# Two u buffers with products spread over the steps, and another order of work from step 95 on, in a kernel of long convolution and a rational-activation MLP

## The chip, the cores and the metric

The kernel runs on one core of one Trainium2 chip. The metric is the device time of one execution in microseconds; the median of several executions stands for a kernel. The profile and the trace come from one execution that the hardware profiler recorded.

## The reference

Two stages follow each other. The first is a long convolution along the sequence, gated twice; the second is an MLP whose activation is a ratio of two polynomials of h and |h|:

```python
h_mlp = np.maximum(pos_emb @ w1, 0.0) @ w2          # (12480, 128)
h_filt = h_mlp * np.exp(-0.01 * pos)[:, None]
u = x * v                                           # (2, 12480, 128)
y = irfft(rfft(u, 2*S, axis=1) * rfft(h_filt, 2*S, axis=0), 2*S, axis=1)[:, :S]
x2 = (x * y).reshape(B * S, D)                      # 24960 rows of 128

h = x2 @ w_in                                       # d_ff = 2048
P = a[0] + a[1]*h + a[2]*h**2 + a[3]*h**3
Q = 1.0 + abs(b[0])*abs(h) + abs(b[1])*h**2
out = (P / (Q + 1e-06)) @ w_out
```

## The kernel before, in words

The convolution is done as transforms on TensorE. The first part of the program (up to about 370 us) makes the filter's spectrum and the whole convolution of batch 0. The second part, `second_part`, runs the MLP over both batches and, beside the MLP of batch 0, the convolution of batch 1.

The MLP's rows are cut into 52 tiles: per batch two halves of 12 tiles of 5 residues (5 x 98 = 490 rows) and one of 4 (392 rows; the narrow tile, every thirteenth). The 2048 hidden units of a tile are done in four parts, so there are 208 steps s = (tile j, part c). A step has four pieces of 128 hidden units, in two halves i = 0, 1 of two pieces each. For a step, the short way of computing (the one that runs here) does this:

- TensorE: `mm1` (L870 to L872) makes half i of h in PSUM, two banks, one per piece; the pool `hp` has two such tiles, one per half in turn.
- ScalarE: `act_v` (L904) makes (h + s)^2 into `v`; `act_q` (L880) makes |h| into `q`; both per half. `act_sq` (L932) squares all four pieces of `q` in place; `act_ln` (L948) takes the logarithm of all four into `l` (one buffer); `act_exp` (L953) makes the first estimate of the reciprocal, per half, into `r` in PSUM (one buffer, two banks).
- VectorE: `dve_v` (L914) finishes the cubic from `v` and h, per half, and is the last reader of that half of h; `dve_e` (L959) and `dve_n` (L964) do one Newton step with `r`, per half.
- GpSimd: `pool_p` (L969) adds a constant to the whole of `v`; `pool_g` (L975) multiplies `v` by `q`, per half.
- TensorE: `mm2` (L987) multiplies by `wout` and adds into `acc`; after the fourth part `store` copies `acc` out on VectorE (L998, L1001) and SyncE's queue writes it.

`q` has three buffers, `v` four. The order of instructions on every engine is written by hand: the string `FIRST` lists the works of a step, each with a delay in steps, and a loop sorts all works of all steps by `s - delay + i / len(order)`. Names end in the half: `d0-1` is `dve_v` of half 0, one step late. `s0`, `s1`, `s2` are three slots per step, in which `slot` does one piece of other work: three of a tile's twelve slots prepare the next tile's input (`attn_a` twice, whose products are L822 on VectorE; `attn_b`, whose cast and difference are L840 and L841), the others run `conv_step`. `tk` takes up what a slot has filled in PSUM.

The convolution of batch 1 goes in 64 groups of two channels, each with three items: s1 (reads u; additions on GpSimd), s2 (product with the spectrum `hg`), s3 (ScalarE copies `qt`, L217, and GpSimd makes `ys`). Its input u = x * v is made in four quarters of 32 channels, `uq`, one buffer. A quarter is eight products on GpSimd (`mult_quarter`, L244) of pieces `xq` and `vq` that SyncE's queue loads (four buffers each), after a memset (`quarter`, L239). `load_step`, called in every slot, does up to two products per call, a next quarter only when all s1 items of the quarter before have been issued; s1 waits in `conv_step` until its quarter is full and READY calls have passed. `load_y` forces the convolution to its end before it is read, about step 97.

`act_q2`, `dve_q3`, `act_sq3` and `pool_q3` are defined and listed in `work`, but no name in `FIRST` calls them:

```python
def act_q2(s):      # ScalarE: |h| of piece 2
def dve_q3(s):      # VectorE: |h| of piece 3, as integer AND 0x7FFFFFFF, PSUM to SBUF
def act_sq3(s):     # ScalarE: square of q, pieces 0 to 2
def pool_q3(s):     # GpSimd: q = q + dl (one input), then q = q * q, piece 3
```

Of the kernel before, what the change touches and what calls it, by code (L numbers as in the profile page):

```python
# [20 lines left out]
N2 = 128  # L21
# [14 lines left out]
UQ = 32  # L36
UC = 16
# [6 lines left out]
CS = 2  # L44
# [4 lines left out]
FIRST = (  # L49
    "v0+0 d1-1 tk+0 m21-3 ln-1 e1-2 q0+0 s1-1 p-1 n1-2 x0-1 m11+0 "  # L50
    "g1-2 q1+0 s2-1 st-3 v1+0 d0+0 tk+0 e0-1 sq+0 m20-2 n0-1 x1-1 "
    "g0-1 s0+0 m10+1 "
)

ATTN = ((1, 2, 4), (1, 3, 5))

# [48 lines left out]
def build(ctx: ExitStack, tc, x, v, pos_emb, w1, w2, w_in, w_out, moe_a, moe_b,  # L105
# [21 lines left out]
    def load_rows(dst, src, t0, k, c0, c, pad, queue=nc.sync):  # L127


        h = N2 // 2  # L130
        if t0 < h < t0 + k:
            load_rows(dst[:, 0:h - t0], src, t0, h - t0, c0, c, pad, queue)
            load_rows(dst[:, h - t0:k], src, h, t0 + k - h, c0, c, pad, queue)
        elif t0 < h:
            queue.dma_start(out=dst[0:M], in_=rows(src, 0, M, t0, k, c0, c))
        else:
            queue.dma_start(out=dst[0:96], in_=rows(src, 0, 96, t0, k, c0, c))
            if pad:
                a = rows(src, 96, 1, t0, k, c0, c)
                queue.dma_start(out=dst[96:98], in_=bass.AP(a.tensor, a.offset, [[0, 2]] + [list(p) for p in a.ap[1:]]))  # L140
            else:
                queue.dma_start(out=dst[96:97], in_=rows(src, 96, 1, t0, k, c0, c))
# [86 lines left out]
    def load_quarter(pool, b, q, n0, bufs):  # L229
        c0 = q * UQ  # L230
        xt = pool.tile([M, UC, UQ], F32, tag="xq", name="xq", bufs=bufs)
        vt = pool.tile([M, UC, UQ], F32, tag="vq", name="vq", bufs=bufs)
        load_rows(xt, xb[b], n0, UC, c0, UQ, False)
        load_rows(vt, vb[b], n0, UC, c0, UQ, True)
        return xt, vt

    def quarter(pool, name, bufs):
        u = pool.tile([M, UQ, N2], F32, tag=name[:2], name=name, bufs=bufs)
        nc.gpsimd.memset(u[96:98, :, H2:], 0.0)  # L239
        return u  # L240

    def mult_quarter(engine, u, n0, xt, vt):
        k = M if n0 < H2 else M - 1
        engine.tensor_tensor(  # L244
            out=u[0:k, :, n0:n0 + UC].rearrange("p c t -> p t c"), in0=xt[0:k], in1=vt[0:k], op=ALU.mult)
# [11 lines left out]
    with ExitStack() as st:  # L257
# [34 lines left out]
        us, uw = {}, []  # L292
# [353 lines left out]
    def second_part(short):  # L646
        st = ExitStack()
# [5 lines left out]
        up = st.enter_context(tc.tile_pool(name="up", bufs=1, reuse_waits="tile"))  # L653
# [57 lines left out]
        us = []  # L711
        pieces = [(q, n0) for q in range(D // UQ) for n0 in range(0, N2, UC)]
        coming = []
        s1_done = [0]

        def load_step():
            for p in us:
                p[2] += p[1] == 0
            for _ in range(2):
                if coming and coming[0][0] * (UQ // CS) <= s1_done[0]:  # L720
                    q, n0, xt, vt = coming.pop(0)
                    if q == len(us):
                        us.append([quarter(up, f"uq{q}", 1), N2 // UC, 0])
                    mult_quarter(nc.gpsimd, us[q][0], n0, xt, vt)
                    us[q][1] -= 1
            while pieces and len(coming) < 4:
                q, n0 = pieces.pop(0)
                coming.append((q, n0) + load_quarter(up, 1, q, n0, 4))

        items = conv_items()  # L730
        item = [next(items)]
# [2 lines left out]
        def take_up():  # L734
            if taken[0] is not None:
                fn, t = taken[0]
                taken[0] = None
                fn(t)
# [7 lines left out]
        def conv_step(now):  # L746
            if item[0] is None:
                return
            kind, ready, fetch, work = item[0]
            if kind != now:  # L750
                return
            if ready is not None and not ready():
                return
            if fetch is not None:
                fetch()
            issue(*work)
            item[0] = next(items, None)
# [7 lines left out]
        def load_y(j):  # L765
            if j >= len(tiles):
                return
            b, p0, _ = tiles[j]
            p0 = chunk(p0)
            if (b, p0) in yc:  # L770
                return
            while b and item[0] is not None:
                load_step()
                conv_step(item[0][0])
            take_up()
            n = min(YC, H2 - p0 % H2)
            t = mp.tile([K1, NY, 2, YC, CY], F32, tag="yc", name="yc", bufs=1)
            o = 0 if j else NPT
            nc.sync.dma_start(out=t[:, :, :, o:n, :].rearrange("p g r t c -> p g r (t c)"),
                              in_=y_d[b][:, :, :, p0 + o:p0 + n, :].rearrange("p g r t c -> p g r (t c)"))  # L780
            yc[b, p0] = t
# [8 lines left out]
        def load_xg(j):  # L790
            if j >= len(tiles):
                return
            b, p0, n = tiles[j]
            xt = mp.tile([M, NPT, D], F32, tag="xt", name="xt", bufs=2)
            load_rows(xt[:, 0:n], xb[b], residue(p0, n), n, 0, D, True)
            gt = mp.tile([K1, NPT, 2, M], F32, tag="gt", name="gt", bufs=2)
            nc.sync.dma_start(out=gt[:, 0:n], in_=g_d[:, p0:p0 + n])
            xg[j] = (xt, gt)
# [5 lines left out]
        def attn_a(j, q):  # L804

            b, p0, n = tiles[j]
            yt = yc[b, chunk(p0)] if j else y0
            xt, gt = xg[j]
            i0 = q * NA
            i1 = min(n, i0 + NA)  # L810

            def fill(cv):
                for i in range(i0, i1):
                    k = i if p0 < H2 else n - 1 - i
                    for r in range(2):
                        nc.tensor.matmul(out=cv[0:M, 0, (i - i0) * D:(i - i0 + 1) * D], lhsT=gt[:, k, r, :],  # L816
                                         rhs=yt[:, :, r, p0 - chunk(p0) + k, :], start=(r == 0), stop=(r == 1))

            def take(cv):
                if q == 0:  # L820
                    an[j] = mp.tile([M, NPT, D], F32, tag="an", name="an", bufs=1)
                nc.vector.tensor_tensor(  # L822
                    out=an[j][:, i0:i1, :], in0=cv[0:M, 0, 0:(i1 - i0) * D].rearrange("p (t c) -> p t c", c=D),
                    in1=xt[:, i0:i1, :], op=ALU.mult)
            issue(fill, take)

        def attn_b(j):
            n = tiles[j][2]
            w = n * M
            take_up()  # L830
            t = an.pop(j)

            def fill(cv):
                for i in range(n):
                    nc.tensor.transpose(out=cv[:, 0, i * M:(i + 1) * M], in_=t[:, i, :], identity=ident[0:M, 0:M])

            def take(cv):
                hi = mp.tile([D, NPT * M], F32R, tag="ahi", name="ahi", bufs=2)
                lo = mp.tile([D, NPT * M], F32R, tag="alo", name="alo", bufs=2)
                nc.vector.tensor_copy(out=hi[:, 0:w], in_=cv[:, 0, 0:w])  # L840
                nc.vector.tensor_tensor(out=lo[:, 0:w], in0=cv[:, 0, 0:w], in1=hi[:, 0:w].bitcast(F32), op=ALU.subtract)  # L841
                ah[j] = (hi, lo)
            issue(fill, take)
# [170 lines left out]

        def slot(s, k):

            load_step()
            j, c = steps[s]
            i = 3 * c + k
            if i == 0:  # L1020
                at[:] = ATTN[item[0] is None]
            if j + 1 < len(tiles) and i in at:
                q = at.index(i)
                if q == 2:
                    attn_b(j + 1)
                else:
                    attn_a(j + 1, q)
                return
            take_up()
            if i == at[2] + 1:  # L1030
                load_xg(j + 2)
                load_y(j + 2)
            conv_step((i - sum(i > k for k in at)) % 3)
# [19 lines left out]
                "qa": act_q2, "qd": dve_q3, "sr": act_sq3, "pq": pool_q3}  # L1053
        plan = []
        for s in range(ns):
            order = FIRST.split()
            for i, w in enumerate(order):
                name, delay = w[:-2], int(w[-2:])
                plan.append((s - delay + i / len(order), s, name))
        for _, s, name in sorted(plan):  # L1060
            if name in work:
                work[name](s)
# [4 lines left out]
    with tc.If(rv > 0) as cmp:  # L1067
        second_part(True)
    with cmp.Else():
        second_part(False)  # L1070
# [26 lines left out]
```

## Time and profile before

| | us |
|---|---|
| median of 3 runs | 2366.91 (2366.55 to 2369.27) |
| profiled execution | 2364.71 |
| its span | 2362.9 |
| TensorE matmul busy | 2038.9 (86%) |
| VectorE busy | 2033.5 (86%) |
| ScalarE busy | 2028.6 (86%) |
| GpSimd busy | 1827.9 (77%) |
| mean granted TensorE clock | 0.97 |

In the rows below, PE is TensorE, DVE VectorE, ACT ScalarE and POOL GpSimd; L followed by a number is a line of the kernel. A row of a window gives the busy time of each engine in a stretch of the span, in microseconds, with the number of instructions. A row of the timeline gives an instruction's start and duration, and in brackets the idle time before it and what ended that. A row of grouped instructions gives their number, busy time, and the mean of one in nanoseconds. Instructions of one engine overlap a little at their ends, so what one costs in a row of others is the distance of the starts.

### The profile page before, as it was taken

What the parts mean: (1) busy time and instruction counts of PE and PEld (TensorE: products, weight loads), DVE (VectorE), ACT (ScalarE), POOL (GpSimd) and SP (SyncE); (2) the same over time, 40 slices, a digit from 0 to 9 for tenths busy, and PEclk for the clock granted to TensorE, in tenths of its full rate; (3) what the DMA queues carried; (4) which work ended last, traced back from release to release, by engine and by line L of the source; (5) the groups of instructions that cost most, each with busy time, mean ns of one, the idle gap of its engine ahead of it and who ended that gap; (6) DMA issues with size and microseconds to landing.
All of it is one profiled execution on the core that took longest, in us unless ns stands there. A gap on an engine that the chain in (4) does not pass through costs nothing.

```text
span 2362.9 us, 35120 instructions
## 1 busy us (share of the span) xinstructions
PE 2038.9 (86%) x13344; PEld 1799.9 (76%) x13344; DVE 2033.5 (86%) x2261; ACT 2028.6 (86%) x1971; POOL 1827.9 (77%) x1274
## 2 busy tenths in 40 slices
PE   6899886999899989998999898887788878877787
PEld 4677774888788878887888777776777767777775
DVE  7999984899799978998999888888888888888886
ACT  5322225999899989998999999999999999999997
POOL 4588765899899998999999766667666766767666
PEclk9999997999999999999999999999999999999999
DMA  7465428322522262314321201212021122120210
GB/s 151 102 148 131 119 76 136 75 63 66 99 66 60 64 102 60 76 54 93 74 63 43 54 21 40 45 31 45 17 44 38 27 44 45 31 45 15 46 24 10
DMA packets 357834, 150.20 MB, mean 64 GB/s; under 512 B 292518, under 2 KB 339880, under 8 KB 354776
## 3 DMA queue, kind: packets, MB, share of 16 engines
q1 hardware_dynamic: 350632, 124.10, 25.9%
q10 hardware_dynamic: 7024, 23.76, 3.2%
q8 instruction: 107, 1.75, 0.3%
q14 instruction: 71, 0.58, 0.1%
HBM read 99.65 MB, written 48.17 MB: 63 GB/s over the span
## 4 chain that ended last, share of the span: by engine, by line
ACT 57%; PE 16%; DVE 15%; POOL 5%; issue 4%; DMA 2%; SPq 1%; DVEq 0%; POOLq 0%; ACTq 0%
ACT v L904 13%; ACT q L880 12%; ACT l L948 11%; ACT r L953 11%; ACT q L932 9%; PE acc L987 4%; DVE v L914 2%; DVE q L959 2%; PE cv L816 2%; DVE q L964 2%; PE cs L582 2%; PE cs L150 2%; POOL v L975 1%; PE h L870 1%; PE h L871 1%
## 5 line engine op out<-in xcount | busy, mean ns | idle before, releaser
L975 POOL TENSOR_TENSOR v<-v,q 128x980 f32<-128x980 f32 (+1 forms) x416 | 936.6, 2252 | 356.1 <-DVE q L964 346.4
L987 PE MATMUL acc<-wout,v 128*128 128x128 f32 (+2 forms) x6656 | 845.4, 280 | 79.5 <-DVE ot L1001 48.1
L987 PEld LDWEIGHTS acc<-wout,v 128*128 128x128 f32 (+2 forms) x6656 | 803.0, 190 | 126.8 <-POOL v L969 53.1
L914 DVE SCALAR_TENSOR_TENSOR v<-v,sc,h 128x980 f32<-128x980 f32 (+1 forms) x416 | 505.2, 1214 | 138.1 <-ACT q L880 132.2
L959 DVE SCALAR_TENSOR_TENSOR q<-q,sc,r 128x980 f32<-128x980 f32 (+1 forms) x416 | 504.9, 1214 | 73.8 <-ACT r L953 73.7
L964 DVE SCALAR_TENSOR_TENSOR q<-q,r 128x980 f32<-128x980 f32 (+1 forms) x416 | 482.2, 1159 | 14.4
L870 PE MATMUL h<-ahi,win_l 128*128 128x490 f32 (+1 forms) x832 | 366.7, 441 | 143.3 <-DVE v L914 138.3
L904 ACT ACTIVATE v<-h,sc 128x980 f32<-128x980 f32 (+1 forms) x416 | 454.4, 1092 | 33.2 <-PE h L872 31.4
L880 ACT ACTIVATE q<-h 128x980 f32<-128x980 f32 (+1 forms) x416 | 415.0, 998 | 20.0 <-PE h L872 14.1
L953 ACT ACTIVATE r<-l 128x980 f32<-128x980 f32 (+1 forms) x416 | 418.4, 1006 | 12.5 <-DVE q L964 12.5
L932 ACT ACTIVATE q<-q,sc 128x1960 f32<-128x1960 f32 (+1 forms) x208 | 404.8, 1946 | 0.0
L948 ACT ACTIVATE l<-q,sc 128x1960 f32<-128x1960 f32 (+1 forms) x208 | 400.9, 1928 | 0.0
L969 POOL TENSOR_SCALAR v<-v,sc 128x1960 f32<-128x1960 f32 (+1 forms) x208 | 392.8, 1888 | 0.1
L871 PE MATMUL h<-alo,win_h 128*128 128x490 f32 (+1 forms) x832 | 324.5, 390 | 0.0
L872 PE MATMUL h<-ahi,win_h 128*128 128x490 f32 (+1 forms) x832 | 323.3, 389 | 0.0
L870 PEld LDWEIGHTS h<-ahi,win_l 128*128 128x128 f32 x832 | 160.6, 193 | 187.0 <-DVE v L914 134.3
L872 PEld LDWEIGHTS h<-ahi,win_h 128*128 128x128 f32 x832 | 161.2, 194 | 26.8
L871 PEld LDWEIGHTS h<-alo,win_h 128*128 128x128 f32 x832 | 161.8, 195 | 14.0 <-DVE alo L841 0.4
L816 PE MATMUL cv<-yc,gt 90*98 90x128 f32 x1004 | 127.8, 274 | 1.5 <-DVE ta L162 0.9
L816 PEld LDWEIGHTS cv<-yc,gt 90*98 90x98 f32 x1004 | 117.4, 166 | 5.7 <-DVE an L822 1.3
L589 ACT ACTIVATE qt<-cs 90x512 f32<-90x512 f32 x64 | 34.5, 589 | 97.9 <-PE cs L582 97.9
L582 PEld LDWEIGHTS cs<-idfth,yy 128*90 128x90 f32 x512 | 61.2, 165 | 32.5 <-issue 25.5
(110 smaller groups left out, 2346.3 us busy)
## 6 DMA issues: line engine op xcount, KB each, us to landing
yc<-y_d SPq DMA_DIRECT2D x23, 900.0 KB
gt<-in_g_dram SPq DMA_DIRECT2D x48, 344.5 KB
h_d<-hg ACTq DMA_DIRECT2D x32, 360.0 KB
y_d<-ys ACTq DMA_DIRECT2D x16, 720.0 KB
hg<-h_d SPq DMA_DIRECT2D x64, 180.0 KB
y_d<-ys SPq DMA_DIRECT2D x16, 720.0 KB
xq<-in_x_dram SPq DMA_DIRECT2D x32, 196.0 KB
vq<-in_v_dram SPq DMA_DIRECT2D x32, 196.0 KB
```

Source lines behind the costliest of these rows:

```text
L870: nc.tensor.matmul(out=t[:, k, 0:w], lhsT=wl, rhs=hi[:, 0:w], start=True, stop=False)
L871: nc.tensor.matmul(out=t[:, k, 0:w], lhsT=wh, rhs=lo[:, 0:w], start=False, stop=False)
L880: nc.scalar.activation(out=halves(st_q[s], i, width(s)), in_=st_h[s, i], func=AF.Abs, **({} if short else {"scale": col("b0")}))
L904: nc.scalar.activation(out=v, in_=st_h[s, i], func=AF.Square, bias=col("s"))
L914: stt(out=v, in0=v, scalar=col("k"), in1=h, op0=ALU.add, op1=ALU.mult)
L932: nc.scalar.activation(out=q, in_=q, func=AF.Square, bias=col("dl"))
L948: nc.scalar.activation(out=part(st_l, s, i), in_=part(st_q, s, i), func=AF.Ln, **({"bias": col("ka")} if short else {}))
L953: nc.scalar.activation(out=t[:, :, 0:w], in_=halves(st_l[s], i, w), func=AF.Exp, scale=-1.0)
L959: nc.vector.scalar_tensor_tensor(out=q, in0=q, scalar=col("ka") if short else 0.0, in1=st_r[s, i], op0=ALU.add, op1=ALU.mult)
L964: nc.vector.scalar_tensor_tensor(out=q, in0=q, scalar=2.0, in1=st_r.pop((s, i)), op0=ALU.subtract, op1=ALU.mult)
L975: nc.gpsimd.tensor_tensor(out=v, in0=v, in1=halves(st_q[s], i, w), op=ALU.mult)
L987: nc.tensor.matmul(out=acc[j][0:k, q // 128, :], lhsT=g[:, i, q:q + k], rhs=wout[:, f, :], start=(f == 0 and q == 0), stop=(f == NF - 1), ...
```

## The change

It adds a second string, `REST`, that holds for the steps from 95 on, moved by 1.875 steps against `FIRST`. In `REST` the second abs is split: ScalarE does piece 2 (`qa`), VectorE piece 3 (`qd`); ScalarE squares pieces 0 to 2 (`sr`), GpSimd piece 3 (`pq`, two instructions); `pool_p` is done in two halves (`p0`, `p1`). The order of the works on every engine is another one; ScalarE's is qa, x0, sr, v1, v0 of the next step, x1, q0 of the next step, ln. Up to step 94 `FIRST` stays. `uq` gets a second buffer, so that a quarter may be filled while the quarter before is still read; after the first quarter, products come one a step (slot 0) instead of two a slot; `xq` and `vq` have three buffers instead of four.

```diff
+REST = (
+    "g0-2 e1-2 p0-1 qa+0 s1+1 n1-2 d0+0 g1-2 qd+0 x0-1 p1-1 e0-1 "
+    "m20-2 m10+1 s2+1 pq+0 sr+0 v1+0 n0-1 d1+0 s0+2 v0+1 m21-2 x1-1 "
+    "q0+1 tk+0 m11+1 tk+0 ln+0 st-2 "
+)
+SHIFT, SWITCH = 1.875, 95
...
-        def load_step():
+        def load_step(k=0):
             for p in us:
                 p[2] += p[1] == 0
-            for _ in range(2):
-                if coming and coming[0][0] * (UQ // CS) <= s1_done[0]:
+            for _ in range(2 if not us or us[0][1] else int(k == 0)):
+                if coming and (coming[0][0] - 1) * (UQ // CS) <= s1_done[0]:
                     q, n0, xt, vt = coming.pop(0)
                     if q == len(us):
-                        us.append([quarter(up, f"uq{q}", 1), N2 // UC, 0])
+                        us.append([quarter(up, f"uq{q}", 2), N2 // UC, 0])
                     mult_quarter(nc.gpsimd, us[q][0], n0, xt, vt)
                     us[q][1] -= 1
-            while pieces and len(coming) < 4:
+            while pieces and len(coming) < 3:
                 q, n0 = pieces.pop(0)
-                coming.append((q, n0) + load_quarter(up, 1, q, n0, 4))
+                coming.append((q, n0) + load_quarter(up, 1, q, n0, 3))
...
         def slot(s, k):
-            load_step()
+            load_step(k)
...
         for s in range(ns):
-            order = FIRST.split()
+            order, shift = (FIRST, 0) if s < SWITCH else (REST, SHIFT)
+            order = order.split()
             for i, w in enumerate(order):
                 name, delay = w[:-2], int(w[-2:])
-                plan.append((s - delay + i / len(order), s, name))
+                plan.append((s - delay + shift + i / len(order), s, name))
```

## Rows read from the trace of the kernel before

**Rows 1.** Windows: eleven wide tiles, and step 95 to the last logarithm; columns as printed.

```profile
core 0: us, PE busy (x) PEld busy (x) DVE busy (x) ACT busy (x) POOL busy (x), PEclk, DMA share, GB/s
...
1325.83:2343.00 1017.17, 834.97 (x5576) 745.20 (x5576) 852.50 (x836) 1006.97 (x896) 707.33 (x336) 0.97 0.16 34
1402.48:1809.86 407.38, 331.99 (x2207) 298.30 (x2206) 341.24 (x331) 403.38 (x353) 282.19 (x133) 0.97 0.17 36
```

**Rows 2.** Timeline of ScalarE in one step: start, duration (us), instruction.

```profile
1800.76 1.94 ACT L948 ACTIVATE l<-q,sc 128x1960 f32<-128x1960 f32 x1
1802.57 1.00 ACT L880 ACTIVATE q<-h 128x980 f32<-128x980 f32 x1
1803.44 1.01 ACT L953 ACTIVATE r<-l 128x980 f32<-128x980 f32 x1
1804.35 1.01 ACT L880 ACTIVATE q<-h 128x980 f32<-128x980 f32 x1
1805.21 1.11 ACT L904 ACTIVATE v<-h,sc 128x980 f32<-128x980 f32 x1
1806.17 1.97 ACT L932 ACTIVATE q<-q,sc 128x1960 f32<-128x1960 f32 x1
1807.99 1.03 ACT L953 ACTIVATE r<-l 128x980 f32<-128x980 f32 x1
```

**Rows 3.** Timeline of VectorE in the same step.

```profile
1803.60 1.23 DVE L914 SCALAR_TENSOR_TENSOR v<-v,sc,h 128x980 f32<-128x980 f32 x1 [1.25 <-ACT q L880]
1804.75 1.23 DVE L959 SCALAR_TENSOR_TENSOR q<-q,sc,r 128x980 f32<-128x980 f32 x1
1806.02 1.17 DVE L964 SCALAR_TENSOR_TENSOR q<-q,r 128x980 f32<-128x980 f32 x1
1807.11 1.23 DVE L914 SCALAR_TENSOR_TENSOR v<-v,sc,h 128x980 f32<-128x980 f32 x1
```

**Rows 4.** Windows: the three refills of u, then fifteen plain steps with convolution.

```profile
622.92:651.75 28.83, 21.16 (x133) 19.27 (x134) 17.12 (x20) 18.72 (x18) 24.78 (x18) 0.88 0.95 144
851.65:868.45 16.80, 10.68 (x50) 9.51 (x51) 8.78 (x9) 8.34 (x9) 16.80 (x15) 0.70 0.89 124
1071.01:1087.31 16.30, 11.18 (x67) 9.68 (x68) 11.46 (x13) 9.85 (x11) 16.30 (x14) 0.90 0.96 164
918.39:1061.64 143.25, 137.84 (x978) 126.83 (x979) 134.84 (x135) 142.92 (x133) 134.34 (x114) 1.00 0.23 58
```

**Rows 5.** Groups of GpSimd instructions by shape, whole run: busy us, mean ns, idle before.

```profile
L975 POOL TENSOR_TENSOR v<-v,q 128x980 f32<-128x980 f32 x384 | 876.9, 2284 | 327.4 <-DVE q L964 318.1 <-ACT q L932 5.8
L969 POOL TENSOR_SCALAR v<-v,sc 128x1960 f32<-128x1960 f32 x192 | 367.6, 1915 | 0.1
L244 POOL TENSOR_TENSOR uq<-xq,vq 97x512 f32<-97x512 f32 x16 | 20.3, 1299 | 4.1 <-DMA vq<-in_v_dram 4.1
L455 POOL TENSOR_TENSOR win_l<-f,win_h 128x256 fp32r<-128x256 f32 x8 | 15.2, 1902 | 1.4 <-ACT win_h L460 1.4
L239 POOL MEMSET uq<- 2x2048 f32 x4 | 7.2, 1802 | 0.2
```

**Rows 6.** ScalarE's copy of `qt`, grouped by shape, 389 to 1330 us.

```profile
L217 ACT ACTIVATE qt<-cv 90x512 f32<-90x512 f32 x64 | 39.3, 615 | 0.0
```

**Rows 7.** VectorE's passes for the next tile and the store, by shape, from 1400 us.

```profile
L841 DVE TENSOR_TENSOR alo<-cv,ahi 128x490 fp32r<-128x490 f32 x23 | 15.4, 669 | 0.8
L840 DVE CAST ahi<-cv 128x490 fp32r<-128x490 f32 x23 | 15.2, 661 | 0.0
L998 DVE COPY ot<-acc 128x384 f32<-128x384 f32 x26 | 14.3, 549 | 0.0
L822 DVE TENSOR_TENSOR an<-cv,xt 98x384 f32<-98x384 f32 x25 | 13.7, 549 | 0.0
L822 DVE TENSOR_TENSOR an<-cv,xt 98x256 f32<-98x256 f32 x23 | 9.6, 416 | 0.0
L1001 DVE COPY ot<-acc 106x128 f32<-106x128 f32 x24 | 6.7, 280 | 0.0
```

**Rows 8.** Waits in all, 1600 to 2000 us: us in total, times, longest.

```profile
DVE v L914 <- ACT q L880: 41.2, 43, 1.3
```

## The prediction

> **What bounds the kernel now.** I read the windows by stage first, then one step on ScalarE and VectorE, then the waits. A step is one pass of the loop over (tile, quarter of the hidden units). Its logarithm on ScalarE (L948) marks it, and I count steps by that. From step 104 to 148, eleven wide tiles, 407.38 us pass: 37.03 a tile, 9.26 a step, and ScalarE is busy 403.38 of them [rows 1]. VectorE has 341.24 (7.76 a step) and GpSimd 282.19 (6.41), so GpSimd idles 2.85 us a step. From step 95 to the last logarithm it is 1017.17 us for 112 steps, ScalarE busy 1006.97.
>
> ScalarE's step in order of time [rows 2] has its instructions start one right behind the other: logarithm 1.81 (1800.76 to 1802.57), abs 0.87, exp 0.91, abs 0.86, square of h 0.96, square of q 1.82, exp 0.91, and the square of h again 0.96: 9.10 in all. Four such steps are 36.4, so a tile loses about 0.6 to waits. What ScalarE does is what a step costs. On VectorE [rows 3] the passes follow each other after 1.15 (`dve_v`), 1.27 (`dve_e`) and 1.09 (`dve_n`), twice a step: 7.02.
>
> In the first 95 steps ScalarE also copies `qt` for the convolution of batch 1. Fifteen plain steps there take 143.25 us, 9.55 each, and GpSimd is busy 134.34 of them, so only 0.59 a step is spare [rows 4]. Three short stretches are much longer: 28.83 us for two steps, 16.80 and 16.30 for one each. In them ScalarE is busy only 18.72, 8.34 and 9.85, while GpSimd works almost throughout (24.78, 16.80, 16.30) [rows 4]: the single `uq` buffer is refilled, eight products of 1.30 us and a memset of 1.80 [rows 5], all in one burst in front of the step's own GpSimd work.
>
> **The change, part by part.** *ScalarE, from step 95.* The second abs falls from two pieces to one, the square of q from four to three. A ScalarE pass over 512 columns (`qt`) takes 615 ns [rows 6] against 1.00 for 980 [rows 2], which starts the next after 0.87; so 0.46 for one piece, 0.40 saved. A quarter of 1.82 is 0.455. Together 0.85; with no fixed cost at all it would be 0.89, and 0.70 if the whole 0.615 of the short pass counts. ScalarE's step is then 8.25, a tile 33.0.
>
> *VectorE, from step 95.* One more pass, 490 columns from PSUM to SBUF as integers. No row shows that operation. The cast of 490 columns from PSUM takes 661 ns, a two-input pass of 490 takes 669 [rows 7]; below, half of the 1.09 that a 980-column pass needs, 0.55; above, the 1.23 of a whole one. I take 0.66, of which 0.08 overlaps the next: 0.58. VectorE's step is 7.60. Per tile come two products (0.55 and 0.42), a cast and a difference (0.66 and 0.67) and the store's copies (0.55 and 0.28) [rows 7]: 3.13, about 2.65 with overlap. A tile on VectorE is then 30.4 + 2.65 = 33.05. **The two engines become equal.** By the new order both products fall into one step (about 8.4), the cast pair into the next (8.80), the copies into a third (8.27), and the fourth is ScalarE's 8.25. If nothing carries over between steps, that is 33.7; if all does, 33.05. Today's order loses 0.6 a tile although VectorE has spare time, so I lean to the upper end and take 33.9.
>
> *GpSimd, from step 95.* A one-input pass over 490 (a quarter of 1.92: 0.48) and a product (half of 2.28: 1.14) [rows 5]: 1.62. Its two half additions instead of one whole add next to nothing. 6.41 + 1.62 = 8.03, inside 8.25 to 8.5. The cover is its idle time, which is nearly used up. The logarithm now waits for this square too. In the new order VectorE's abs stands right behind the first `dve_v`, the GpSimd square follows after `p1`, and by the gaps above it ends more than a microsecond ahead of the logarithm; I cost the wait at nothing. If GpSimd is late, ScalarE's whole queue stands behind the logarithm.
>
> The Trainium skill speaks against this move: "GPSIMD Engine Reference", section "Engine selection", has VectorE do elementwise work because GpSimd is about half as fast with two inputs. By that the square belongs on VectorE, where about 0.6 more would make VectorE's step 8.2 and its tile some 35.5; the rows decide for GpSimd, because here it has 2.85 us free and VectorE has not.
>
> *A new wait in PSUM.* VectorE waited 41.2 us, 43 times of up to 1.3, with `dve_v` for ScalarE's abs [rows 8], though it uses nothing of that abs: what they share is the h tile. So readers of one bank go one after the other, in program order. "PSUM — Partial Sum Buffer" of the Trainium skill, section "PSUM bank collisions raise a hardware error", says that two engines must not touch one bank in the same cycle, reads included; the wait agrees. Hence ScalarE's `v1`, which reads both pieces, now waits for VectorE's abs. In steady state x1's end, then `e1`, `n1`, the first `dve_v` and the abs (1.27 + 1.09 + 1.15 + 0.66 = 4.2) must fit ahead of `v1`, while ScalarE does q0, logarithm, abs, exp and square of q (0.87 + 1.81 + 0.46 + 0.91 + 1.37 = 5.4). About a microsecond is left; the cast pair (1.33) uses it up in one step of four. TensorE's next h product, queued behind, has as much room.
>
> *Sum from step 95.* 112 steps are 25 wide tiles and 3 narrow ones. 37.03 - 33.9 = 3.13, times 25: 78. For narrow ones, whose fixed costs don't shrink, I take half, 1.5 each: 4.5. Together **83 us less**. Ends: 33.05 a tile gives 105, 35.2 (8.80 in every step) gives 48. The switch itself, where the pipeline is laid anew, I put at 3 us; at most one step, 9, at least 0.
>
> *The second buffer.* The first quarter's fill is unchanged: two products a call, and DMA decides. The other three refills cost today 28.83 - 19.10 = 9.7, then 7.25 and 6.75: 23.7 us. Afterwards the same work per quarter (8 x 1.30 + 1.80 = 12.2) comes one product a step. Eight steps have 8 x 0.59 = 4.7 to spare; 7.5 is left over. The bursts of today also bring 12.2 and stall for 7.9 on average, so the queue soaks up 4.3, some 0.9 of it spare time; 3.4 is slack of the buffers. The refill then still stalls for about 4, once less because the convolution has barely begun. Together some 10, so **14 us less**, between 1 (no slack, 3 x 7.5) and 24. The loads come three ahead instead of four, and at one piece a step that is three steps ahead; behind them on SP's queue stand `hg`, `xt`, `gt` and the stores, which were behind the bursts before. I cost that at nothing. The convolution ends some steps earlier, its sum unchanged.
>
> *Sum.* 83 + 14 - 3 = 94. The profiled execution took 2364.71 us (span 2362.9), the median of the runs is 2366.91, 2.2 above. I take the difference off the median: **2273 us**.
>
> **Rivals.** *(a) The two engines alternate instead of overlapping.* `r` has one buffer: exp, `dve_e`, `dve_n`, exp. With VectorE full, each late `dve_n` holds ScalarE, and every step becomes as long as the worst, 8.80: 48 + 14 - 3 = 59, 2308 us. For: a tile loses 0.6 today already. Against: without extras VectorE has 0.65 to spare.
>
> *(b) The second buffer brings nothing.* GpSimd lacks the time however the products are spread, stalls only move: 83 + 1 - 3 = 81, 2286 us. For: 0.59 spare a step against 1.3. Against: the burst hits the buffers' slack once, the spread uses eight steps.
>
> *(c) The abs holds `v1` in every step* [rows 8], TensorE's next h product comes late, and ScalarE stays near 9.2: only the buffer counts, 2353 us. Against: the microsecond worked out above.
>
> *(d) Slower.* GpSimd becomes the bound at the new square. A two-input pass on 256 elements took 1.90 in the weight split (L455) [rows 5], three times the rate of `pool_g`; at that rate 490 cost 3.64, with the addition 4.12. A step is then 6.41 + 4.12 = 10.5, 1.27 longer than 9.26: 112 x 1.27 = 142 more, less 14, 2495 us. It decides from 2.85 us for the two new instructions on. Against: that row writes the rounded type; `pool_g`, float like the square, is the nearer one.
>
> **Chances.** Forecast 0.56, (a) 0.20, (b) 0.14, (c) 0.05, (d) 0.05. The range takes in the forecast's ends and (a) and (b): 2246 (33.05 a tile and most of the buffer's gain, 105 + 17 - 1 = 121) to 2313 ((a) with 9 for the switch, 59 - 6 = 53). Outside are (c), (d) and the far ends. Faster by over 0.2% (about what a measurement of this kernel tells from no change) 0.93, within it 0.02, slower 0.05.
>
> **What would show it.** Late tiles of 33.5 to 34.2 us between logarithms; ScalarE busy 8.2 a step, VectorE's share up from 84% to about 98% and GpSimd's from 69% to about 95%; an integer pass of about 0.66 on VectorE; square and addition on GpSimd at 1.6 together; no long burst of `uq` products, and steps of about 10 instead of 16 while a quarter is filled. Wrong would be: ScalarE idle over 0.5 a step in front of the logarithm (GpSimd late), `v1` (abs late) or the exps (a); or GpSimd above 8.3 a step (d).

## The result, and the profile after

The changed kernel takes 2274.71 us (median; 2271.58 to 2275.97), the one before 2366.73 in the same comparison: ratio 0.9608, 95% interval 0.9594 to 0.9623, so 92 us less. The forecast was 2273 with a range of 2246 to 2313. The profiled execution took 2275.51, its span is 2273.6; against that of before 89 us less. In the changed kernel's profile every line below the new string stands six lines later (L948 of before is L954); the new L948 and L949 are GpSimd's two instructions, L899 is VectorE's abs, L893 and L943 are ScalarE's abs of one piece and square of three.

Windows of the changed kernel, in the columns of [rows 1]. First 44 steps of wide tiles (from step 105) and step 95 to the last logarithm, as [rows 1]; then, as [rows 4], steps 24 to 26, which are plain, step 27, step 47 and fifteen plain steps; last, step 94.

```profile
core 0: us, PE busy (x) PEld busy (x) DVE busy (x) ACT busy (x) POOL busy (x), PEclk, DMA share, GB/s
...
1403.72:1771.85 368.13, 325.05 (x2208) 280.94 (x2207) 360.89 (x375) 367.76 (x354) 363.87 (x265) 1.00 0.19 40
1322.24:2252.40 930.16, 818.62 (x5528) 702.64 (x5528) 900.97 (x945) 919.75 (x896) 908.37 (x669) 1.00 0.17 37
624.94:653.50 28.56, 27.54 (x195) 24.62 (x194) 27.18 (x29) 28.47 (x28) 28.42 (x24) 1.00 0.53 96
653.50:669.55 16.05, 12.10 (x68) 11.34 (x67) 9.31 (x10) 9.84 (x10) 16.05 (x15) 0.79 0.59 122
850.73:865.17 14.44, 10.52 (x72) 10.20 (x71) 8.77 (x9) 9.04 (x10) 14.44 (x14) 0.88 0.55 106
914.25:1057.57 143.32, 137.85 (x977) 126.80 (x978) 134.88 (x135) 142.98 (x133) 134.40 (x114) 1.00 0.25 63
1303.90:1322.24 18.34, 16.17 (x104) 14.78 (x104) 11.12 (x12) 10.66 (x10) 13.87 (x9) 0.91 0.26 47
```

The 112 late steps fell from 1017.17 to 930.16, 87.0 less; a wide tile from 37.03 to 33.47 (368.13 / 11). In it ScalarE is busy 99.9%, GpSimd 98.8% and VectorE 98.0% of the time: three engines end within 2% of each other. Step 94, where one order gives way to the other, takes 18.34 instead of 9.12. The plain steps of the convolution are what they were (143.32 against 143.25). Of the long steps of the refills two are left, 27 and 47, with GpSimd working throughout; a third no longer appears.

One late step, first on ScalarE, then on GpSimd (timeline: start, duration; the x2 are v1 and the next step's v0).

```profile
1420.35 1.97 ACT L954 ACTIVATE l<-q,sc 128x1960 f32<-128x1960 f32 x1
1422.17 0.62 ACT L893 ACTIVATE q<-h 128x490 f32<-128x490 f32 x1
1422.63 1.04 ACT L959 ACTIVATE r<-l 128x980 f32<-128x980 f32 x1
1423.54 1.57 ACT L943 ACTIVATE q<-q,sc 128x1470 f32<-128x1470 f32 x1
1424.96 2.09 ACT L910 ACTIVATE v<-h,sc 128x980 f32<-128x980 f32 x2
1426.88 1.05 ACT L959 ACTIVATE r<-l 128x980 f32<-128x980 f32 x1
1427.79 1.05 ACT L886 ACTIVATE q<-h 128x980 f32<-128x980 f32 x1
1428.66 1.99 ACT L954 ACTIVATE l<-q,sc 128x1960 f32<-128x1960 f32 x1
```

```profile
1417.70 0.70 POOL L948 TENSOR_SCALAR q<-q,sc 128x490 f32<-128x490 f32 x1
1418.48 1.00 POOL L949 TENSOR_TENSOR q<-q 128x490 f32<-128x490 f32 x1
1419.44 2.30 POOL L981 TENSOR_TENSOR v<-v,q 128x980 f32<-128x980 f32 x1
1421.71 1.09 POOL L975 TENSOR_SCALAR v<-v,sc 128x980 f32<-128x980 f32 x1
1422.76 2.32 POOL L981 TENSOR_TENSOR v<-v,q 128x980 f32<-128x980 f32 x1
1425.03 1.11 POOL L975 TENSOR_SCALAR v<-v,sc 128x980 f32<-128x980 f32 x1
1426.09 0.71 POOL L948 TENSOR_SCALAR q<-q,sc 128x490 f32<-128x490 f32 x1
```

ScalarE starts one instruction right behind the other, 8.31 from logarithm to logarithm (against 9.10 in [rows 2]): the abs of one piece costs 0.46, the square of three 1.42. GpSimd too has no gap over 0.08, and its round, from 1417.70 to 1426.09, is 8.39. That is **longer than ScalarE's**. Up to step 134 most steps take 8.30, and in each of them GpSimd falls behind by 0.09, of which the one step of 8.49 in a tile gives 0.1 back: at step 109 its square ends 0.88 ahead of the logarithm that reads it, at step 135 only 0.10. By then the slack is used up, and the four steps from 135 on take 8.40, 8.39, 8.46 and 8.31, together 33.56, which is four of GpSimd's rounds. The narrow tile gives the slack back (the lead is 2.78 at step 155), and the same begins again. Four rows of step 135 show how GpSimd holds ScalarE (timeline of each engine; the last is v0 of the next step):

```profile
1654.29 2.30 POOL L981 TENSOR_TENSOR v<-v,q 128x980 f32<-128x980 f32 x1
1656.65 2.04 PE L993 MATMUL acc<-wout,v 128*128 128x128 f32 x16 [1.02 <-POOL v L981]
1659.65 0.38 PE L878 MATMUL h<-ahi,win_h 128*128 128x490 f32 x1
1660.08 1.08 ACT L910 ACTIVATE v<-h,sc 128x980 f32<-128x980 f32 x1
```

TensorE stands idle for 1.02 until GpSimd's product is there, and makes the next h only behind that product's multiplication. That h ends at 1660.03, and ScalarE's v0, which reads it, starts 1.04 behind v1 instead of 0.96. So GpSimd reaches ScalarE through TensorE's queue. The delay is not idle time in the rows, because ScalarE's instructions overlap by about 0.1; a busy share of 99.9% therefore does not prove that nothing waits.

Grouped by shape, in late steps (GpSimd 1400 to 1780 us; VectorE to 2250): number, busy us, mean ns.

```profile
L975 POOL TENSOR_SCALAR v<-v,sc 128x980 f32<-128x980 f32 x91 | 99.0, 1088 | 0.0
L949 POOL TENSOR_TENSOR q<-q 128x490 f32<-128x490 f32 x46 | 46.1, 1003 | 3.8
L948 POOL TENSOR_SCALAR q<-q,sc 128x490 f32<-128x490 f32 x46 | 31.6, 688 | 0.0
```

```profile
L899 DVE TENSOR_SCALAR q<-h 128x490 int32<-128x490 int32 x94 | 62.1, 660 | 0.2 <-ACT q L893 0.2
```

VectorE's abs has the length of the cast it was costed by [rows 7], 0.66. GpSimd's addition on a quarter is 0.69, not the 0.48 of a quarter of 1.92; its square 1.00, not 1.14; and two half additions to `v` take 2 x 1.09 where one whole took 1.92 [rows 5].

### The profile page after: what moved, and what is told of

It is laid out like the page before. It is cut to its first block, busy times and chain, and to the rows that moved or that the text cites. A ratio compares the mean times of both kernels' runs of the same rounds, so it can differ in the third digit from the quotient of the medians.

```text
span 2273.6 us, 35833 instructions
## 1 busy us (share of the span) xinstructions
PE 2026.0 (89%) x13344; PEld 1758.5 (77%) x13344; DVE 2083.5 (92%) x2374; ACT 1942.7 (85%) x1971; POOL 2037.5 (90%) x1613
## 4 chain that ended last, share of the span: by engine, by line
POOL 36%; ACT 25%; PE 22%; DVE 10%; issue 3%; DMA 2%; SPq 2%; POOLq 0%; DVEq 0%; ACTq 0%
POOL v L981 19%; POOL v L975 9%; PE acc L993 6%; ACT v L910 6%; ACT l L954 5%; ACT r L959 5%; ACT q L886 4%; POOL q L949 4%; ACT q L938 3%; POOL q L948 2%; PE cv L822 2%; PE cs L588 2%; PE cs L156 2%; PE h L876 2%; PE h L877 2%
## 5 line engine op out<-in xcount | busy, mean ns | idle before, releaser
L993 PEld LDWEIGHTS acc<-wout,v 128*128 128x128 f32 (+2 forms) x6656 | 774.3, 186 | 193.7 <-POOL v L981 168.4
L910 ACT ACTIVATE v<-h,sc 128x980 f32<-128x980 f32 (+1 forms) x416 | 438.5, 1084 | 31.6 <-PE h L878 30.3
L975 POOL TENSOR_SCALAR v<-v,sc 128x980 f32<-128x980 f32 (+3 forms) x321 | 422.7, 1317 | 0.0
L954 ACT ACTIVATE l<-q,sc 128x1960 f32<-128x1960 f32 (+1 forms) x208 | 401.3, 1929 | 0.9 <-POOL q L949 0.7
L876 PE MATMUL h<-ahi,win_l 128*128 128x490 f32 (+1 forms) x832 | 360.6, 433 | 29.7 <-DVE v L920 27.2
L877 PE MATMUL h<-alo,win_h 128*128 128x490 f32 (+1 forms) x832 | 319.5, 384 | 0.0
L878 PE MATMUL h<-ahi,win_h 128*128 128x490 f32 (+1 forms) x832 | 317.4, 382 | 0.0
L886 ACT ACTIVATE q<-h 128x980 f32<-128x980 f32 (+1 forms) x303 | 302.6, 999 | 8.9 <-PE h L878 6.2
L938 ACT ACTIVATE q<-q,sc 128x1960 f32<-128x1960 f32 (+1 forms) x95 | 185.8, 1955 | 0.0
L943 ACT ACTIVATE q<-q,sc 128x1470 f32<-128x1470 f32 (+1 forms) x113 | 170.9, 1513 | 0.0
L949 POOL TENSOR_TENSOR q<-q 128x490 f32<-128x490 f32 (+1 forms) x113 | 111.4, 986 | 9.4
```

Of the source, the lines that this page charges most:

```text
L876: nc.tensor.matmul(out=t[:, k, 0:w], lhsT=wl, rhs=hi[:, 0:w], start=True, stop=False)
L877: nc.tensor.matmul(out=t[:, k, 0:w], lhsT=wh, rhs=lo[:, 0:w], start=False, stop=False)
L878: nc.tensor.matmul(out=t[:, k, 0:w], lhsT=wh, rhs=hi[:, 0:w], start=False, stop=True)
L910: nc.scalar.activation(out=v, in_=st_h[s, i], func=AF.Square, bias=col("s"))
L954: nc.scalar.activation(out=part(st_l, s, i), in_=part(st_q, s, i), func=AF.Ln, **({"bias": col("ka")} if short else {}))
L975: nc.gpsimd.tensor_scalar(out=v, in0=v, scalar1=col("p0" if short else "a0"), scalar2=1.0, op0=ALU.add, op1=ALU.mult)
```

## The experiments

### The two halves of the change by themselves

Only the buffers:

```diff
-SHIFT, SWITCH = 1.875, 95
+SHIFT, SWITCH = 1.875, 208
```

> Only the buffers and the spread products; the order of work is the old one to the end. Theory (the buffer gives about 13 us, the order about 87 less 9 at the switch): 2367 - 13 = 2354 us; late tiles 37.0 as before, the long steps 27 and 47 as in the changed kernel. Rival (the second buffer brings nothing, stalls only move): 2365 to 2367.

Measured: 2351.87 us against 2367.45, ratio 0.9934 (0.9917 to 0.9950), 15.6 less. Steps 27 and 47 take 15.99 and 13.88, a late tile 37.04, with the same four steps as before (9.12, 9.11, 9.11, 9.70). The buffer does what was forecast, and the rival falls.

Only the order:

```diff
-            for _ in range(2 if not us or us[0][1] else int(k == 0)):
-                if coming and (coming[0][0] - 1) * (UQ // CS) <= s1_done[0]:
+            for _ in range(2):
+                if coming and coming[0][0] * (UQ // CS) <= s1_done[0]:
...
-                        us.append([quarter(up, f"uq{q}", 2), N2 // UC, 0])
+                        us.append([quarter(up, f"uq{q}", 1), N2 // UC, 0])
...
-            while pieces and len(coming) < 3:
+            while pieces and len(coming) < 4:
...
-                coming.append((q, n0) + load_quarter(up, 1, q, n0, 3))
+                coming.append((q, n0) + load_quarter(up, 1, q, n0, 4))
```

> Only the new order from step 95; one u buffer and bursts of products as before. Theory: 2367 - 87 + 9 = 2289 us, late tiles 33.5, the three long refills of before (28.8, 16.8, 16.3) back. Rival (the order needs the earlier end of the convolution, so that steps 95 on are disturbed): above 2295.

Measured: 2289.76 us, ratio 0.9669 (0.9652 to 0.9685), 77.7 less; step 94 takes 17.94, the next 8.29 and 8.30, so the order does not need the earlier end of the convolution. The long refills are back (27.94 for two steps, then 15.78 and 16.48). 15.6 + 77.7 = 93.3 against 92.0 for both: the halves add, neither needs the other.

### What the step at the switch is made of

```diff
-SHIFT, SWITCH = 1.875, 95
+SHIFT, SWITCH = 0.875, 95
```

> The changed kernel with the new order moved by 0.875 steps instead of 1.875, so that its first works stand one step earlier in every queue. Theory (step 94 takes 18.3 instead of 9.1 because the h product of step 95 stands on TensorE behind the last products of steps 93 and 94, which wait for GpSimd): most of the 9 us goes, 2275 - 6 = 2269, between 2266 and 2272. Rival (the 9 us is the price of filling the new pipeline, wherever it starts): 2275, the same; or the later works are now in the way and it is slower.

Measured: 2271.24 us (2268.29 to 2273.02), 3.5 less than the changed kernel, at the upper edge of what the theory gave; the ranges of the two kernels' runs overlap a little, so the total alone does not settle it. The windows are plainer: steps 93 to 95, in the changed kernel and then here.

```profile
1295.00:1330.54 35.54, 25.47 (x156) 23.06 (x154) 26.16 (x29) 27.46 (x26) 22.88 (x15) 0.88 0.39 74
```

```profile
1292.64:1322.69 30.05, 25.50 (x162) 23.28 (x161) 26.20 (x29) 27.46 (x27) 23.34 (x15) 0.89 0.45 88
```

The same work, ScalarE busy 27.46 in both, in 5.5 us less. ScalarE's idle time in these three steps falls from 8.1 to 2.6. So a good half of the 9 us came from where the first works of the new order stand in the queues, and the rest stays. What stands in the way is what the theory said: in step 94 of the changed kernel TensorE's first product for h starts only at 1311.24, behind two groups of `mm2` that waited 2.36 and 0.63 for GpSimd, and ScalarE waits 4.5 us for h in that step, against 1.3 in these three steps with the earlier start.

### Whether the long steps are GpSimd's load

```diff
-            for _ in range(2 if not us or us[0][1] else int(k == 0)):
+            for _ in range(2 if not us or us[0][1] else int(k == 0 and s % 2 == 0)):
```

(with s handed to `load_step` by `slot`)

> The changed kernel with a product of u only in every second step after the first quarter. Theory (GpSimd has 0.59 us a step to spare, a product takes 1.3, so that one a step overfills it and one in two steps does not quite, with the buffers' slack of 3 to 4 us per quarter): steps 27 and 47 fall from 16.0 and 14.4 to below 11, together 9 to 11 us, 2265 us. Rival (the long steps come from something else than GpSimd's load, such as the stores and loads on SyncE's queue, 9.9 us for eight stores at step 26): they stay, 2275.

Measured: 2265.09 us, ratio 0.9570 (0.9554 to 0.9586), 9.6 less than the changed kernel. Windows of steps 26 and 27, and of 47:

```profile
641.56:660.75 19.19, 18.61 (x130) 16.98 (x129) 18.11 (x17) 19.19 (x20) 19.19 (x19) 1.00 0.37 84
841.53:850.43 8.90, 8.05 (x60) 7.41 (x58) 8.16 (x9) 8.81 (x10) 8.90 (x9) 1.00 0.00 0
```

Both long steps are gone. GpSimd works throughout steps 26 and 27 and ScalarE too: the load only just fits. The stores on SyncE's queue are unchanged, so they were not the cause. The loads of pieces come half as often as well, but in the changed kernel GpSimd worked throughout step 27 (16.05 of 16.05) and did not wait for them. Steps 50 and 51, at the narrow tile with convolution, take 10.20 and 10.10 here as in the changed kernel, with ScalarE waiting for h: that is not the refill. Steps 48 and 49 ahead of them take 10.23 and 10.40 here instead of 9.12 and 8.88, so of the 5.5 saved at step 47 2.6 come back.

### Whose time a late step is

*No work moved, the new order kept:*

```diff
-    "g0-2 e1-2 p0-1 qa+0 s1+1 n1-2 d0+0 g1-2 qd+0 x0-1 p1-1 e0-1 "
-    "m20-2 m10+1 s2+1 pq+0 sr+0 v1+0 n0-1 d1+0 s0+2 v0+1 m21-2 x1-1 "
+    "g0-2 e1-2 p0-1 q1+0 s1+1 n1-2 d0+0 g1-2 x0-1 p1-1 e0-1 "
+    "m20-2 m10+1 s2+1 sq+0 v1+0 n0-1 d1+0 s0+2 v0+1 m21-2 x1-1 "
```

> The changed kernel, its new order from step 95, but no work moved: ScalarE does the abs of both pieces and the square of all four, VectorE's abs and GpSimd's two instructions are gone. Theory (a late step costs what ScalarE does in it, 8.30 with the moved work): 8.30 + 0.40 + 0.455 = 9.15 a step, 112 x 0.85 = 95 more, 2370 us. Rival (part of the gain is the order itself, shorter waits between the engines): 2330 to 2350.

Measured: 2350.85 us, between the two forecasts and next to the rival's. The step is what the theory gave, 9.11, with ScalarE busy without a gap:

```profile
1408.00:1800.00 392.00, 314.29 (x2159) 279.24 (x2157) 334.39 (x321) 392.00 (x344) 287.31 (x172) 1.00 0.18 37
```

But the tile's slip is gone: 36.55 (9.22, 9.11, 9.12, 9.11) where the old order with the same work took 37.03. That is the order's own part: the 112 late steps take 1004.9 against 1017.2, so 12.3 of the 87.0 are the order and 74.7 the moved work. Step 94, 20.20 here, takes 11 back; hence the same time as with the buffers alone (2351.87). My sum of 95 was also too large because the changed kernel's late tiles are longer than four times 8.30, and because narrow tiles gain little: steps 98 to 103 take 49.28 here and 48.27 in the changed kernel.

*The abs back on ScalarE:*

```diff
-                nc.vector.tensor_scalar(out=q.bitcast(I32), in0=h.bitcast(I32), scalar1=0x7FFFFFFF, scalar2=None,
-                                        op0=ALU.bitwise_and)
+                nc.scalar.activation(out=q, in_=h, func=AF.Abs)
```

> The changed kernel with the abs of the last piece on ScalarE, as a pass of its own; the square stays on GpSimd. Theory (ScalarE binds): 8.30 + 0.46 = 8.76 a step, 45 to 52 us more, 2322 us, and GpSimd and VectorE get idle time. Rival (GpSimd at 8.27 us binds as much, ScalarE's 0.46 is partly hidden): less than 20 more.

Measured: 2317.41 us (2314.41 to 2320.40), 42.7 more, steps of 8.76 to 8.85.

```profile
1404.01:1780.00 375.99, 319.00 (x2157) 277.07 (x2156) 331.51 (x320) 375.99 (x386) 355.23 (x258) 1.00 0.18 39
```

ScalarE 375.99 of 375.99; the others have room. Here ScalarE alone binds, and the 0.46 shows whole in the step (8.30 to 8.76). The total is a little under the forecast, since the changed kernel lost some to GpSimd.

*The square on VectorE:*

```diff
-                nc.gpsimd.tensor_scalar(out=q, in0=q, scalar1=col("dl"), scalar2=1.0, op0=ALU.add, op1=ALU.mult)
-                nc.gpsimd.tensor_tensor(out=q, in0=q, in1=q, op=ALU.mult)
+                nc.vector.tensor_scalar(out=q, in0=q, scalar1=col("dl"), scalar2=1.0, op0=ALU.add, op1=ALU.mult)
+                nc.vector.tensor_tensor(out=q, in0=q, in1=q, op=ALU.mult)
```

> The changed kernel with the addition and the square of the last piece on VectorE instead of GpSimd. Theory (VectorE is busy 8.20 of 8.37 us a step and has no room): 0.3 for the addition and 0.6 for the square more, 9.1 a step, 2275 + 112 x 0.75 = 2359 us. Rival (elementwise work is better on VectorE, as the Trainium skill's table of engines has it, since GpSimd is full at 8.27): at most 2290.

Measured: 2407.0 us, ratio 1.0170 (1.0149 to 1.0190) to the kernel before: slower than that. VectorE becomes the bound:

```profile
1410.33:1800.00 389.67, 306.67 (x2031) 273.36 (x2029) 385.64 (x423) 343.08 (x324) 270.50 (x163) 0.96 0.16 33
```

Its two new passes, grouped by shape over the same stretch:

```profile
L948 DVE TENSOR_SCALAR q<-q,sc 128x490 f32<-128x490 f32 x40 | 34.7, 867 | 0.0
L949 DVE TENSOR_TENSOR q<-q 128x490 f32<-128x490 f32 x40 | 26.8, 670 | 1.4
```

The rule of the Trainium skill ("GPSIMD Engine Reference", section "Engine selection") that elementwise work goes to VectorE does not hold here, where VectorE is the fuller engine. It cost more than forecast because the addition took 0.87, not 0.3; 0.47 of that is the pass, the rest a wait for GpSimd (last section). Without that wait VectorE's step would be, by estimate, 8.20 (360.89 / 44, above) + 0.47 + 0.67 = 9.34, still no shorter than the 9.26 of before.

*GpSimd a little less, GpSimd a little more:*

```diff
-    "g0-2 e1-2 p0-1 qa+0 s1+1 n1-2 d0+0 g1-2 qd+0 x0-1 p1-1 e0-1 "
+    "g0-2 e1-2 p-1 qa+0 s1+1 n1-2 d0+0 g1-2 qd+0 x0-1 e0-1 "
```

> The changed kernel with GpSimd's addition to v in one instruction of 1960 instead of two of 980, in the place of the first. Two take 1.09 each, one took 1.92, so GpSimd does 8.0 instead of 8.27 a step. Theory (ScalarE binds, GpSimd is just inside): the same, 2271 to 2277. Rival (GpSimd binds in the steps of 8.4, the slips of a tile are its): a tile falls from 33.5 towards 33.2, 7 us less, 2268.

```diff
                 nc.gpsimd.tensor_scalar(out=q, in0=q, scalar1=col("dl"), scalar2=1.0, op0=ALU.add, op1=ALU.mult)
+                nc.gpsimd.tensor_scalar(out=q, in0=q, scalar1=0.0, scalar2=1.0, op0=ALU.add, op1=ALU.mult)
```

> The changed kernel with one more GpSimd instruction per step from 95 on: an addition of 0 to the last piece (0.69 us) between the addition and the square. Theory (ScalarE, VectorE and GpSimd are within 0.2 us of each other; GpSimd at 8.27 binds as soon as it gets more): 8.27 + 0.69 = 8.96 a step, 112 x 0.6 = 66 more, 2341 us, GpSimd busy throughout. Rival (GpSimd still has room beside ScalarE): at most 2295.

Measured: 2266.64 us with the whole addition (ratio 0.9581, 0.9565 to 0.9597), 8.1 less than the changed kernel: here the rival was right. Late tiles take 33.39 (8.49 and three of 8.30) throughout, without the steps of 8.40.

```profile
1400.64:1767.00 366.36, 322.27 (x2203) 284.31 (x2201) 359.54 (x372) 366.12 (x352) 354.77 (x221) 1.00 0.19 40
```

GpSimd has 11.6 us to spare in 366 and ScalarE 0.2. TensorE's waits for GpSimd's product, 1400 to 1800 us, in the changed kernel and then here (in all, times, longest):

```profile
PEld acc L993 <- POOL v L981: 62.7, 62, 2.0
```

```profile
PEld acc L993 <- POOL v L981: 4.3, 14, 0.8
```

In the two traces the 112 late steps differ by 6.5 (930.1 and 923.6), and 4.8 of that lie at the narrow tiles (steps 98 to 103, 150 to 155 and 202 to 206). There the steps get shorter while GpSimd still takes 8.39: steps 98 and 99 of the changed kernel take 7.98 and 7.62, and the square's lead on the logarithm falls from 0.94 to 0.03 by step 100.

With one more instruction it is 2350.79 us, 76 more than the changed kernel, with steps of 9.02 on average (8.3 to 10.1). ScalarE waits for L950, GpSimd's square, in front of its logarithm (12.7 us in 26 times, 1400 to 1800 us), and as long again for h, which TensorE makes late behind GpSimd's product. The wait that I had costed at nothing comes to life here. GpSimd binds with what it was given, and the changed kernel stands just past that point.

### The abs behind v1 instead of ahead of it

```diff
-    "g0-2 e1-2 p0-1 qa+0 s1+1 n1-2 d0+0 g1-2 qd+0 x0-1 p1-1 e0-1 "
-    "m20-2 m10+1 s2+1 pq+0 sr+0 v1+0 n0-1 d1+0 s0+2 v0+1 m21-2 x1-1 "
+    "g0-2 e1-2 p0-1 qa+0 s1+1 n1-2 d0+0 g1-2 x0-1 p1-1 e0-1 "
+    "m20-2 m10+1 s2+1 sr+0 v1+0 qd+0 pq+0 n0-1 d1+0 s0+2 v0+1 m21-2 x1-1 "
```

> The changed kernel with VectorE's abs of the last piece, and GpSimd's two instructions on it, behind ScalarE's v1 in the order instead of ahead of it. Theory (readers of one PSUM tile go one after the other in program order; behind v1 the abs starts only when v1 has ended, between dve_e and dve_n, and the second exp waits for both): about a microsecond a step, 2275 + 112 = 2387 us, ScalarE's exps waiting for dve_n. Rival (the wait of v1 for the abs costs as much where it is now): 2260 to 2280.

Measured: 2403.94 us, ratio 1.0152 (1.0132 to 1.0172) to the kernel before. Waits from 1400 to 1800 us (in all, times, longest):

```profile
DVE q L899 <- ACT v L910: 43.3, 39, 1.2
ACT r L959 <- DVE q L970: 42.5, 52, 0.9
POOL q L948 <- DVE q L899: 39.5, 41, 1.4
```

Now the abs waits for v1, 1.1 us a step, `dve_n` stands behind the abs on VectorE, and ScalarE's exps wait for `dve_n`. In this program the readers of a PSUM tile do go one after the other as they are written [rows 8], and where the abs stands decides: 129 us between the two places.

### A version with what was found

Products in every second step, the order moved by 0.875, the addition whole:

> The changed kernel with a product in every second step, the new order moved by 0.875 instead of 1.875, and GpSimd's addition in one instruction. Theory (three separate places, gains add: 10 + 3.5 to 7 + 8): 2253 us, between 2249 and 2256. Rival (they share slack): above 2258.

Measured: 2255.85 us, ratio 0.9525 (0.9509 to 0.9541), 18.9 less than the changed kernel, at the edge of the forecast: the gains nearly add. Of the switch only 4.0 remain saved (steps 93 to 95 take 31.55).

```diff
-SHIFT, SWITCH = 0.875, 95
+SHIFT, SWITCH = 0.875, 92
```

> As the one with all three, and the new order from step 92 instead of 95, right behind the last convolution item. Theory (three steps of 8.3 in place of 9.1): 2.4 us less than that one, 2250. Rival (the last convolution items run into the new order and cost more): the same or slower.

Measured: 2251.06 us, ratio 0.9504 (0.9488 to 0.9520), 4.8 less again, twice the forecast. It beats both kernels: 116.6 us less than the one before in the same comparison (2367.69 - 2251.06).

## Why the prediction was right, point by point

*What binds.* Right for the larger part: a late step was ScalarE's sum. 9.11 with the old work (no work moved), 8.30 with the new, 8.76 with the abs back; ScalarE is idle for 0.1% of the time at most in the three. Where GpSimd's slack was used up (steps 135 to 149, and again from 187 on) it was GpSimd's round of 8.39.

*ScalarE's 8.25.* Measured 8.30: the abs saved 0.40 as forecast, the square 0.40 instead of 0.455.

*VectorE's 7.60 and 0.66.* Right: L899 takes 0.66, and VectorE is 98% busy as forecast. The extras of a tile were carried over better than I took: not 8.4, 8.80, 8.27 but 8.30 and one step of about 8.5. The loss of 0.6 a tile for which I leaned to the upper end belonged to the old order: with no work moved, the new one loses 0.1 (36.55 against four times 9.11). The tile became 33.47 instead of 33.9, and the late steps 87.0 us shorter instead of 83.

*GpSimd's 8.03.* **The term that was mis-sized.** It is 8.39 from round to round. "Two half additions instead of one whole add next to nothing" was wrong, they add 0.25; and a quarter-width addition costs 0.69, not 0.48: I had scaled one-input rows without a fixed part. The square cost 0.14 less than forecast. In a step of 8.25 GpSimd had 8.25 - 6.41 = 1.84 free, not the 2.85 of the old step, and what it was given took 1.98. So it was not inside the step but 0.09 past it, worth the 8.1 us that the whole addition gives back. I saw that its room was "nearly used up", but named VectorE as the equal of ScalarE. "GpSimd above 8.3 a step" stood among my signs of being wrong, and by its round it came.

*The wait of the logarithm for GpSimd's square.* Costed at nothing, and in the changed kernel it cost next to nothing (0.2 us between 1400 and 1800 us). But the lead of "more than a microsecond" had shrunk to 0.10 by step 135. The extra instruction shows this wait to be the next in line. Where GpSimd did hold ScalarE, it did so through TensorE, whose next h stands behind GpSimd's product; the prediction did not have this path.

*The wait of v1 for the abs.* Right where the abs stands: no such wait shows, and in step 135 the abs ends 1.07 ahead of v1 (1657.96 and 1659.03), as forecast. Behind v1 it would have cost 129 us, more than rival (c) gave it.

*The second buffer, 14 us.* 15.6 by itself, with an interval from 11.8 to 19.6. The mechanism holds (one product a step overfills GpSimd, half as many fit). The first refill cost 1.4, spread over steps 8 to 12, the others 6.5 and 4.9 over a plain step, where I had 4 each. The sign "steps of about 10 instead of 16" did not come: each of the two stalls fell into one step, 16.05 and 14.44.

*The switch, 3 us.* Wrong in size: 9.2 (18.34 instead of 9.12), just past the bound of 9 that I gave. I had it filled like any step. More than half of the excess hangs on how far the new order is shifted.

*Sum.* 87 - 9.2 + 15.6 = 93 stands against 83 - 3 + 14 = 94: the errors of +4, -6 and +1.6 cancelled. That the total lies within 2 us of the forecast is luck; the single terms were off by 1.6 to 6.

*The rivals.* (a) fell: 8.37 a step, not 8.80. (b) fell by the buffers alone. (d) did not come, but its price came from a row whose instructions took 0.74 to 2.60 us each, so that one mean was no rate; why they differ so much no run here shows. GpSimd did turn out to be the bound, by 0.09 and not by 2.

## What to carry to other kernels

Where work is moved until several engines are equal, a term of 0.2 us decides which of them binds: cost every split instruction with its fixed part, and take the round from start to start on each engine, not only busy shares. Work that comes in bursts on an engine with little room does better spread at a rate near its spare time: one product of 1.3 us in two steps here, at 0.59 us spare a step, and not one in each. Where one order of work replaces another, look at what the first new instruction stands behind in each queue.

## What the runs showed of the hardware beyond that

VectorE's addition of a scalar in SBUF (L948, the square on VectorE) took 0.47 to 1.02 us for 490 columns, most often 0.98, though it reads one operand. The timeline of that kernel shows why (start, duration):

```profile
1444.22 1.09 POOL L975 TENSOR_SCALAR v<-v,sc 128x980 f32<-128x980 f32 x1
1444.60 0.98 DVE L948 TENSOR_SCALAR q<-q,sc 128x490 f32<-128x490 f32 x1
1445.62 0.67 DVE L949 TENSOR_TENSOR q<-q 128x490 f32<-128x490 f32 x1
```

It ends at 1445.58, 0.27 us after GpSimd's instruction (1445.31). One step later GpSimd's (1453.93, 1.10) ends at 1455.03 and VectorE's (1454.32, 0.98) at 1455.30, again 0.27. Of the 95 such passes from 1390 us on 88 started beside a GpSimd instruction, and all but two ended 0.25 to 0.28 after it; the seven that started with none beside them took 0.47. So it waits, inside its duration, for GpSimd to be done. "SBUF — State Buffer" of the Trainium skill, section "Who interferes with whom", says that VectorE in a two-port mode, which `tensor_scalar` can enter under conditions, and GpSimd share a pair of ports; whichever issues first holds it for its whole instruction and the other blocks. These rows agree. The abs of the change, which reads PSUM, took 0.66 to 0.67 beside GpSimd.

Where GpSimd held TensorE up (the extra instruction), steps such as 113 took 10.03. Windows of steps 112 and 113:

```profile
1470.69:1479.73 9.04, 6.83 (x45) 5.65 (x44) 8.24 (x10) 8.52 (x9) 8.87 (x8) 1.00 0.00 1
1479.73:1489.76 10.03, 7.78 (x44) 7.29 (x45) 7.56 (x8) 8.42 (x8) 9.86 (x8) 0.83 0.32 86
```

The granted clock of step 113 is 0.83 on average, after 1.00 in the two steps before, so TensorE ran part of it at 1.2 GHz instead of 2.4, behind waits of up to 2.8 us for GpSimd's product, and ScalarE then waited 1.6 for h.
